# A long convolution and an MLP on one core: the opening laid out anew

## The chip, the cores and the metric

The kernel runs on one core of one Trainium2 chip. The metric is the device time of one execution in microseconds (us). TensorE is PE in the rows, its weight load PEld, VectorE is DVE, ScalarE is ACT, GpSimd is POOL, SyncE is SP.

## The reference

```python
h_filt = np.maximum(pos_emb @ w1, 0.0) @ w2 * np.exp(-0.01 * pos)[:, None]
u = x * v                                  # (4, 12480, 128)
L = 2 * S
y = irfft(rfft(u, n=L, axis=1) * rfft(h_filt, n=L, axis=0)[None], n=L, axis=1)[:, :S]
z = (x * y).reshape(B * S, D)              # 49920 tokens of 128
h = np.maximum(z @ w_in, 0.0)              # d_ff = 2048
out = (h * h) @ w_out
```

## The kernel before

The sequence is padded to 112 x 112 and the transforms become matrix products. For each of the four batches there are four stages. Stage one (`stage1`) multiplies x and v, folds the product into a sum half and a difference half (the tiles `ut`, three of them) and multiplies them by a small table; a step is four channels, and there are 32 steps. Its result is copied out of PSUM into the large tile `W` (`evac`). Stage two (`stage2`) multiplies each of 56 blocks of `W` by a table (`mm`), giving U in PSUM, and multiplies U by the filter's spectrum as complex numbers, in place in `W` (`post`). Stage three transforms back, 64 steps of two channels (`prep` gathers v out of `W`, `evac` copies to c and writes a sum and a difference into `W`). Stage four does the last transform, multiplies by x and writes z. Each matrix product over fp32 is one `matmul` and two instructions in the trace, in the first stage one for each half of the array's columns.

The filter goes ahead of the batches: an MLP (`filter_mlp`), then stages one and two with `b=None` and `filt=True`. Its spectrum goes through the tile `he` to the DRAM tensor `Hd`, 56 writes of 229 KB, and comes back as `ht` in the first batch's stage two. `Hd`, the inputs `xt` and `vt`, and the tables all go through SP's queue, in the order in which the program issues them.

The filter and the first batch run with `big=True` before the main loop. The other three batches run inside the main loop, spread between the products of the MLP with d_ff = 2048, by a generator from which `adv` takes steps. In the main loop each fp32 product is three of reduced operands: each factor is split into a high and a low part (`mm3`). The weights `w_in` and `w_out` are split the same way from 64-bit values by `convert_weights`, on VectorE with two casts on ScalarE for each piece.

Before the change: the tables of stage two are one tile of 56 blocks (`tabs[0]`), loaded in eight pieces of seven blocks, for the filter during its MLP, for the batch from the last steps of stage one on. The batch's stage one is started early by `step(s1)`: its loads stand at step 4 of the filter's stage one, its first folds three steps before the end of the filter's stage two. The weights are loaded and converted in eight pieces of 512 columns, one `step(conv)` after each step of the batch's stage three. Within each step of a stage the order on the engines is that of the program. `lag` is the number of steps by which `post` or `evac` follows `mm` (two, in stages two and three with `big`).

Of the kernel before, what the change touches and what calls it, by code (L numbers as in the profile page):

```python
# [16 lines left out]
D = 128  # L17
I = 112
# [13 lines left out]
TC = 7  # L32


@with_exitstack
def hyena_moe_kernel(
# [45 lines left out]
    def convert_weights(p, tp, dst):  # L82
        n = 512
        m = DFF // n
        V = nc.vector
        raws = []

        def load(c):
            if c < 2 * m:
                c0 = c % m * n  # L90
                src = w_in if c < m else w_out
                raw = p.tile([128, n, 2], I32, tag="raw", name="raw")
                nc.sync.dma_start(out=raw.rearrange("p a b -> p (a b)"), in_=src.bitcast(I32)[:, c0 * 2 : (c0 + n) * 2])
                raws.append(raw)

        load(0)
        for c in range(2 * m):
            c0, at = c % m * n, c // m * 2
            hi12, lo12 = dst[:, at, c0 : c0 + n], dst[:, at + 1, c0 : c0 + n]
            raw = raws.pop(0)  # L100
            low, high = raw[:, :, 0], raw[:, :, 1]

            def tmp(tag, dt=I32):
                return tp.tile([128, n], dt, tag=tag, name="cv", bufs=2)

            mag, top, sgn, rest = tmp("r", F32), tmp("gh"), tmp("gl"), tmp("r")
            yield
            V.tensor_scalar(out=top, in0=high, scalar1=0x7FFFFFFF, scalar2=None, op0=ALU.bitwise_and)
            V.tensor_scalar(out=mag, in0=top.bitcast(F32), scalar1=2.0**-15, scalar2=122880.0, op0=ALU.max, op1=ALU.min)
            yield  # L110
            V.tensor_scalar(out=top, in0=mag.bitcast(I32), scalar1=3, scalar2=0x7FFFFFFF, op0=ALU.logical_shift_left, op1=ALU.bitwise_and)
            V.tensor_scalar(out=sgn, in0=high, scalar1=-0x80000000, scalar2=0x40000000, op0=ALU.bitwise_and, op1=ALU.bitwise_xor)
            yield
            V.tensor_scalar(out=rest, in0=low, scalar1=1, scalar2=None, op0=ALU.logical_shift_right)
            load(c + 1)
            V.tensor_tensor(out=top, in0=top, in1=sgn, op=ALU.bitwise_xor)
            nc.scalar.copy(mag, rest)
            yield
            tf = top.bitcast(F32)
            V.tensor_scalar(out=sgn, in0=top, scalar1=-0x800000, scalar2=None, op0=ALU.bitwise_and)  # L120
            nc.scalar.copy(hi12, tf)
            yield
            V.scalar_tensor_tensor(out=mag, in0=mag, scalar=2.0**-51, in1=sgn.bitcast(F32), op0=ALU.mult, op1=ALU.mult)
            yield
            V.tensor_sub(out=tf, in0=tf, in1=hi12.bitcast(F32))
            yield
            V.tensor_add(out=lo12, in0=tf, in1=mag)
            yield
# [93 lines left out]
    def stage1(b, big, side="left", hook=None):  # L222
# [4 lines left out]
        with pool("s1", side) as p:  # L227
# [22 lines left out]
            def mul(t):  # L250
# [3 lines left out]
                if filt:  # L254
                    f = first_rows()[:, :, t * DC : (t + 1) * DC].rearrange("p j d -> p d j")
                    eng = nc.vector if t % 4 == 0 or t == 2 else nc.gpsimd
                    eng.tensor_add(out=ut[:, :, :gap], in0=f[:, :, HI:], in1=f[:, :, HI::-1])
                    eng.tensor_sub(out=ut[:, :, 64:], in0=f[:, :, HI + 1 :], in1=f[:, :, HI - 1 :: -1])
                else:
                    xt, vt = L[t]  # L260
                    (nc.vector if big else nc.gpsimd).tensor_mul(out=xt, in0=xt, in1=vt)
                    eng = nc.vector if big and t in (0, 2) else nc.gpsimd
# [20 lines left out]
            def evac(t, A):  # L283
                for h in range(DC // 2):
# [3 lines left out]
                    if big:  # L288
                        (nc.vector.tensor_copy if filt and h else nc.scalar.copy)(view, src)
# [41 lines left out]
    def table(src, k):  # L331
        nc.sync.dma_start(out=tabs[0][:, k * TC : (k + 1) * TC], in_=src[:, k * 2 * TC : (k + 1) * 2 * TC, :].rearrange("p (t k) m -> p t k m", k=2))

    def stage2(filt, big, side="left", hook=None):
# [3 lines left out]
        lh = 5 if big else 0  # L338
        T, Hs = {}, {}

        with pool("s2", side) as p:
# [7 lines left out]
            def load_h(t):  # L349
                if t >= n or filt:  # L350
                    return
                ht = p.tile([I, D, 2, 2], F32, tag="ht", name="ht", bufs=7 if big else 2)
                nc.sync.dma_start(out=ht, in_=Hd[:, t])
                Hs[t] = ht

            def mm(t):
                tb = tabs[0][:, t] if big else T.pop(t)
# [6 lines left out]
            def post(t, U):  # L364
                if filt:
                    he = p.tile([I, D, 4], F32, tag="he", name="he", bufs=4)
                    (nc.vector.tensor_copy if t % 2 else nc.scalar.copy)(he, U[:I].rearrange("p (c d) -> p d c", c=4))
                    nc.sync.dma_start(out=Hd[:, t].rearrange("p d k r -> p (d k r)"), in_=he.rearrange("p d c -> p (d c)"))
                    return
                ht = Hs.pop(t)  # L370
                Uv = U[:I].rearrange("p (k r d) -> p d k r", k=2, r=2)
                m = [
# [7 lines left out]
                eng = nc.vector if big and (t % 4 == 3 or t >= n - 3) else nc.gpsimd  # L380
                eng.tensor_add(out=im[0], in0=im[0], in1=re[1])
# [11 lines left out]
            for t in range(n + lag):  # L393
# [3 lines left out]
                yield 2  # L397
                if t - lag in prev:
# [12 lines left out]
    def stage3(big, ft=None, hook=None):  # L411
        n = D // 2
        with pool("s3") as p:
# [6 lines left out]
            def prep(t):  # L420
# [3 lines left out]
                (nc.gpsimd.tensor_copy if t % (5 if big else 3) == 2 else nc.scalar.copy)(q[t], by_channel(2 * t, 2 * t + 2))  # L424
# [15 lines left out]
            def evac(t, A):  # L440
# [4 lines left out]
                if big and t % 5 == 4:  # L445
                    nc.gpsimd.tensor_add(out=dst[:, 0, :, 1::-1], in0=c[:, :, 3:0:-2], in1=c[:, :, 0:3:2])
                else:
                    nc.vector.tensor_add(out=dst[:, 0, :, 1::-1], in0=q[:, :, 3:0:-2], in1=c[:, :, 0:3:2])
# [149 lines left out]
    ftp = take("ftp")  # L598
    tabs = [take("tbp", "right").tile([KP, NP, 2, I], F32, name="tbl", bufs=1)]

# [71 lines left out]
    def m_h(zT, f):  # L672
        A = psa.tile([128, 2, 512], F32, tag="A", name="A")
        for t in range(2):
            s = slice((2 * f + t) * 128, (2 * f + t + 1) * 128)
            mm3(A[:, t, :GT], (wi[0][:, s], wi[1][:, s]), zT)
# [34 lines left out]
    def m_o(i, f, hl):  # L711
# [4 lines left out]
        for t in range(2):  # L716
            s = slice((2 * f + t) * D, (2 * f + t + 1) * D)
            mm3(o, (wo[0][:, s], wo[1][:, s]), (hl[0][:, t, :], hl[1][:, t, :]), first=(f == 0 and t == 0), last=(f == NS - 1 and t == 1))
# [173 lines left out]
```

## Time and profile before

| what | us |
|---|---|
| median of 3 runs | 3220.01 (3218.57 to 3222.17) |
| the profiled execution | 3218.82 |
| its span | 3217.1 |
| filter MLP (0 to 43 us) | 43 |
| filter stage one (43 to 104) | 61 |
| filter stage two (104 to 153) | 49 |
| batch stage one (153 to 217) | 64 |
| batch stage two (217 to 310) | 93 |
| batch stage three (310 to 413) | 103 |
| start of stage four (413 to 428) | 15 |
| main loop and tail (from 428) | 2789 |

The stretches are cut by hand where the timeline changes from one stage to the next, to about a microsecond; neighbouring stages overlap a little there. In rows of the timeline the first number is the start in us from the span's begin, the second the duration.

### The profile page before, as it was taken

The numbers are of one execution on the slowest core, as the hardware profiler recorded it, in microseconds if no ns is written. First come the engines' busy times: TensorE is split into PE (matmuls) and PEld (weight loads), VectorE is DVE, ScalarE is ACT, GpSimd is POOL, SyncE is SP. The second block draws the span as 40 slices with busy tenths as digits, with TensorE's granted clock in tenths as the row PEclk, the third lists the DMA queues.
The fourth block names the chain that finished last, engine by engine and source line by source line (L and its number), as shares of the span: only waits on it lengthen the run. The fifth ranks groups of instructions, "written<-read, shape, count | busy, mean of one in ns | idle before, by whom it ended". The sixth has DMA issues, their size and how long they took to land.

```text
span 3217.1 us, 51651 instructions
## 1 busy us (share of the span) xinstructions
PE 3109.4 (97%) x17270; PEld 2850.4 (89%) x17270; DVE 2556.1 (79%) x3163; ACT 2412.2 (75%) x3273; POOL 1707.7 (53%) x1765
## 2 busy tenths in 40 slices
PE   8986789999999999999999999999999999999998
PEld 6754679999999999999999999999999999999998
DVE  6449779888887789888887789887887789877776
ACT  4330668778788878778788888778788888888886
POOL 6278956565655556655665566565655566200000
PEclk9999989999999999999999999999999999999999
DMA  5585156433410056534410056433420056300000
GB/s 143 176 214 156 54 126 159 133 97 114 122 58 19 22 138 156 134 100 114 121 56 18 18 138 158 133 104 110 119 64 20 22 125 156 75 25 24 24 26 18
DMA packets 330145, 304.75 MB, mean 95 GB/s; under 512 B 143784, under 2 KB 288472, under 8 KB 329880
## 3 DMA queue, kind: packets, MB, share of 16 engines
q1 hardware_dynamic: 301208, 256.48, 29.2%
q0 software_dynamic: 28672, 44.97, 6.1%
q8 instruction: 137, 2.24, 0.3%
q14 instruction: 128, 1.05, 0.1%
HBM read 215.09 MB, written 63.77 MB: 87 GB/s over the span
## 4 chain that ended last, share of the span: by engine, by line
PE 89%; POOL 3%; DVE 3%; issue 2%; DMA 2%; ACT 1%; SPq 0%; DVEq 0%; POOLq 0%; ACTq 0%
PE A L78 11%; PE A L80 11%; PE A L79 11%; PE O L79 9%; PE O L80 9%; PE O L78 9%; PE F L361 5%; PE F L437 5%; PE F L280 5%; PE F L79 4%; PE F L78 4%; PE F L80 4%; PE A L277 1%; DMA vt<-vs 1%; POOL W L449 1%
## 5 line engine op out<-in xcount | busy, mean ns | idle before, releaser
L687 ACT ACTIVATE r<-A 128x892 f32<-128x892 f32 x896 | 821.7, 917 | 309.5 <-PE A L80 298.8
L78 PE MATMUL A<-zh,wt 128*128 128x446 f32 x1792 | 715.9, 399 | 1.1 <-DVE gl L706 1.0
L706 DVE TENSOR_TENSOR gl<-r,gh 128x892 fp32r<-128x892 f32 x503 | 628.3, 1249 | 87.2 <-ACT r L694 73.6
L80 PE MATMUL A<-zh,wt 128*128 128x446 f32 x1792 | 651.3, 363 | 0.0
L79 PE MATMUL A<-zl,wt 128*128 128x446 f32 x1792 | 650.0, 363 | 0.0
L690 ACT ACTIVATE gh<-r 128x892 fp32r<-128x892 f32 x512 | 486.2, 950 | 141.8 <-PE O L80 128.2
L79 PE MATMUL O<-gl,wt 128*128 128x446 f32 x1440 | 523.8, 364 | 0.4 <-DVE gl L706 0.4
L80 PE MATMUL O<-gh,wt 128*128 128x446 f32 x1440 | 523.1, 363 | 0.0
L78 PE MATMUL O<-gh,wt 128*128 128x446 f32 x1440 | 522.8, 363 | 0.0
L694 ACT ACTIVATE r<-r 128x892 f32<-128x892 f32 x504 | 478.9, 950 | 14.6
L706 DVE TENSOR_TENSOR gl<-A,gh 128x892 fp32r<-128x892 f32 x392 | 426.0, 1087 | 73.6 <-ACT gh L690 55.6
L449 POOL TENSOR_TENSOR W<-c 112x224 f32<-112x224 f32 x256 | 329.9, 1294 | 289.1 <-ACT c L444 288.5
L692 DVE SCALAR_TENSOR_TENSOR A<-A,r 128x892 f32<-128x892 f32 x392 | 424.9, 1084 | 56.7 <-ACT r L687 55.0
L701 DVE CAST gh<-r 128x892 fp32r<-128x892 f32 x384 | 242.8, 632 | 248.5 <-ACT r L694 244.2
L654 POOL TENSOR_TENSOR zl<-zi,zh 128x446 fp32r<-128x446 f32 x111 | 132.4, 1193 | 522.7 <-PE A L80 381.8
L78 PEld LDWEIGHTS A<-zh,wt 128*128 128x128 f32 x1792 | 338.2, 189 | 26.5 <-DVE gl L706 2.6
L79 PEld LDWEIGHTS A<-zl,wt 128*128 128x128 f32 x1792 | 339.6, 190 | 19.6 <-DVE zl L654 0.2
L80 PEld LDWEIGHTS A<-zh,wt 128*128 128x128 f32 x1792 | 336.6, 188 | 22.8
L379 POOL TENSOR_TENSOR W<-W,m 112x256 f32<-112x256 f32 x224 | 217.0, 969 | 211.0 <-DVE m L377 185.1
L508 POOL TENSOR_TENSOR al<-W,ah 112x512 fp32r<-112x512 f32 x212 | 279.3, 1317 | 44.0 <-ACT ah L506 30.9
L79 PEld LDWEIGHTS O<-gl,wt 128*128 128x128 f32 x1440 | 271.8, 189 | 20.2 <-DVE gl L706 1.5
L78 PEld LDWEIGHTS O<-gh,wt 128*128 128x128 f32 x1440 | 270.4, 188 | 18.4
(117 smaller groups left out, 5675.8 us busy)
## 6 DMA issues: line engine op xcount, KB each, us to landing
ht<-Hd SPq DMA_DIRECT2D x224, 224.0 KB
tb<-t POOLq DMA_DIRECT2D x224, 196.0 KB, 3.3
xt<-xs SPq DMA_DIRECT2D x128, 196.0 KB
vt<-vs SPq DMA_DIRECT2D x128, 196.0 KB
xt<-x SPq DMA_DIRECT2D x224, 112.0 KB
out<-ot SPq DMA_DIRECT2D x112, 223.0 KB
tb<-t2s SPq DMA_DIRECT2D x168, 105.0 KB
zd<-zs SPq DMA_DIRECT2D x222, 64.0 KB
```

The source lines that it names most:

```text
L78: nc.tensor.matmul(o, lh, rh, start=first, stop=False)
L79: nc.tensor.matmul(o, lh, rl, start=False, stop=False)
L80: nc.tensor.matmul(o, ll, rh, start=False, stop=last)
L379: nc.gpsimd.tensor_sub(out=re[0], in0=re[0], in1=im[1])
L449: nc.gpsimd.tensor_sub(out=dst[:, 1], in0=c[:, :, 0:3:2], in1=c[:, :, 3:0:-2])
L508: eng.tensor_sub(out=lo, in0=w, in1=hi.bitcast(F32))
L687: nc.scalar.activation(r, h, AF.Relu)
L690: nc.scalar.activation(hi, r, AF.Square)
L692: nc.vector.scalar_tensor_tensor(out=h, in0=h, scalar=0.0, in1=r, op0=ALU.max, op1=ALU.mult)
L694: nc.scalar.activation(r, r, AF.Square)
L701: nc.vector.tensor_copy(hi, g)
L706: nc.vector.tensor_sub(out=lo, in0=g, in1=hi.bitcast(F32))
```

## The change

- `convert_weights`: the 16 pieces of 256 columns are loaded ahead, after the tables of the filter and before its stage one. They are converted in two interleaved chains, three instructions after each step of the filter's stage two. The result goes back into the memory of the raw pieces. Stage three no longer carries it.
- The table tile becomes two of 28 blocks, `tba` and `tbb`. The filter uses both; after its step 27 `tba` is given up and the batch's stage one takes its memory. The batch's stage two uses `tbb` as a ring of four pieces.
- Stage one with `big`: VectorE makes all folds, ScalarE all evacuations.
- Filter stage two: ScalarE makes all copies to `he`, which has three buffers in place of four.
- Batch stage two: ScalarE writes a turned copy of U (i times U) into PSUM, VectorE multiplies U by the real and the turned U by the imaginary part, GpSimd adds the two (VectorE for the last two). `ht` has five buffers in place of seven.
- Batch stage three: VectorE and ScalarE take turns in `prep`; VectorE makes all sums, GpSimd all differences.
- The load of `ft` moves to the front of the program.

```diff
+TH = 4
+CW = 256
+NCW = DFF // CW
...
-    def convert_weights(p, tp, dst):
-        n = 512
...
+    def load_weights(wp):
+        raws = []
+        for c in range(2 * NCW):
+            raw = wp.tile([128, CW, 2], I32, tag="w", name="raw", bufs=2 * NCW)
+            src = (w_in if c < NCW else w_out).bitcast(I32)[:, c % NCW * 2 * CW : (c % NCW + 1) * 2 * CW]
+            nc.sync.dma_start(out=raw.rearrange("p a b -> p (a b)"), in_=src)
+            raws.append(raw)
+        return raws
+
+    def convert_weights(p, wp, raws, wt, chunks):
+        for c in chunks:
+            low, high = raws[c][:, :, 0], raws[c][:, :, 1]
+            mag, top, sgn = (p.tile([128, CW], I32, tag=k, name="cv") for k in ("cm", "ct", "cs"))
+            mf = mag.bitcast(F32)
+            tf = top.bitcast(F32)
+            V.tensor_scalar(out=top, in0=high, scalar1=0x7FFFFFFF, scalar2=None, op0=ALU.bitwise_and)
+            V.tensor_scalar(out=mf, in0=tf, scalar1=2.0**-15, scalar2=122880.0, op0=ALU.max, op1=ALU.min)
+            V.tensor_scalar(out=top, in0=mag, scalar1=3, scalar2=0x7FFFFFFF, op0=ALU.logical_shift_left, op1=ALU.bitwise_and)
+            yield
+            V.tensor_scalar(out=mag, in0=low, scalar1=1, scalar2=None, op0=ALU.logical_shift_right)
+            nc.scalar.copy(mf, mag)
+            yield
+            wt[c] = wp.tile([128, 2, CW], F32R, tag="w", name="wt", bufs=2 * NCW)
+            hi12, lo12 = wt[c][:, 0, :], wt[c][:, 1, :]
+            V.tensor_scalar(out=sgn, in0=top, scalar1=-0x800000, scalar2=None, op0=ALU.bitwise_and)
+            yield
+            V.scalar_tensor_tensor(out=mf, in0=mf, scalar=2.0**-51, in1=sgn.bitcast(F32), op0=ALU.mult, op1=ALU.mult)
+            V.tensor_add(out=lo12, in0=tf, in1=mf)
...
                     f = first_rows()[:, :, t * DC : (t + 1) * DC].rearrange("p j d -> p d j")
-                    eng = nc.vector if t % 4 == 0 or t == 2 else nc.gpsimd
+                    eng = nc.vector
                     eng.tensor_add(out=ut[:, :, :gap], in0=f[:, :, HI:], in1=f[:, :, HI::-1])
                     eng.tensor_sub(out=ut[:, :, 64:], in0=f[:, :, HI + 1 :], in1=f[:, :, HI - 1 :: -1])
...
-                    eng = nc.vector if big and t in (0, 2) else nc.gpsimd
+                    eng = nc.vector if big else nc.gpsimd
                     eng.tensor_add(out=ut[:, :, :HI], in0=xt[:, :, :HI], in1=xt[:, :, HI:])
                     eng.tensor_sub(out=ut[:, :, 64:], in0=xt[:, :, :HI], in1=xt[:, :, HI:])
...
                     if big:
-                        (nc.vector.tensor_copy if filt and h else nc.scalar.copy)(view, src)
+                        nc.scalar.copy(view, src)
...
-    def table(src, k):
-        nc.sync.dma_start(out=tabs[0][:, k * TC : (k + 1) * TC], in_=src[:, k * 2 * TC : (k + 1) * 2 * TC, :].rearrange("p (t k) m -> p t k m", k=2))
+    def table(src, k, half):
+        nc.sync.dma_start(
+            out=half[:, k % TH * TC : (k % TH + 1) * TC],
+            in_=src[:, k * 2 * TC : (k + 1) * 2 * TC, :].rearrange("p (t k) m -> p t k m", k=2),
+        )
...
-        lh = 5 if big else 0
-        T, Hs = {}, {}
+        lh = 4 if big else 0
+        T, Hs, iUs, two = {}, {}, {}, {}
...
-                ht = p.tile([I, D, 2, 2], F32, tag="ht", name="ht", bufs=7 if big else 2)
+                ht = p.tile([I, D, 2, 2], F32, tag="ht", name="ht", bufs=5 if big else 2)
                 nc.sync.dma_start(out=ht, in_=Hd[:, t])
...
-                tb = tabs[0][:, t] if big else T.pop(t)
+                tb = tabs[filt and t < TH * TC][:, t % (TH * TC)] if big else T.pop(t)
...
-                    he = p.tile([I, D, 4], F32, tag="he", name="he", bufs=4)
-                    (nc.vector.tensor_copy if t % 2 else nc.scalar.copy)(he, U[:I].rearrange("p (c d) -> p d c", c=4))
+                    he = p.tile([I, D, 4], F32, tag="he", name="he", bufs=3)
+                    nc.scalar.copy(he, U[:I].rearrange("p (c d) -> p d c", c=4))
                     nc.sync.dma_start(out=Hd[:, t].rearrange("p d k r -> p (d k r)"), in_=he.rearrange("p d c -> p (d c)"))
...
+                if big:
+                    w = W[:I, t].rearrange("p (d k r) -> p d k r", k=2, r=2)
+                    m = p.tile([I, D, 2, 2], F32, tag="m1", name="m1")
+                    iv = iUs.pop(t)[:I].rearrange("p (k r d) -> p d k r", k=2, r=2)
+                    nc.vector.tensor_mul(out=w, in0=Uv, in1=ht[:, :, :, 0:1].to_broadcast([I, D, 2, 2]))
+                    nc.vector.tensor_mul(out=m, in0=iv, in1=ht[:, :, :, 1:2].to_broadcast([I, D, 2, 2]))
+                    (nc.vector if t >= n - 2 else nc.gpsimd).tensor_add(out=w, in0=w, in1=m)
+                    return
...
-                eng = nc.vector if big and (t % 4 == 3 or t >= n - 3) else nc.gpsimd
-                eng.tensor_add(out=im[0], in0=im[0], in1=re[1])
+                nc.gpsimd.tensor_add(out=im[0], in0=im[0], in1=re[1])
+
+            def turn(t, U):
+                if filt or not big:
+                    return
+                if t % 2 == 0:
+                    two[0] = psa.tile([128, 2, 512], F32, tag="A", name="A")
+                iU = iUs[t] = two[0][:, t % 2, :]
+                u, iu = (x[:I].rearrange("p (k r d) -> p k r d", k=2, r=2) for x in (U, iU))
+                nc.scalar.mul(iu[:, :, 0], u[:, :, 1], -1.0)
+                nc.scalar.copy(iu[:, :, 1], u[:, :, 0])
...
+                if t - 1 in prev:
+                    turn(t - 1, prev[t - 1])
                 if t - lag in prev:
                     post(t - lag, prev.pop(t - lag))
                 yield 3
...
-                (nc.gpsimd.tensor_copy if t % (5 if big else 3) == 2 else nc.scalar.copy)(q[t], by_channel(2 * t, 2 * t + 2))
+                copy = (nc.vector.tensor_copy if t % 2 else nc.scalar.copy) if big else nc.gpsimd.tensor_copy if t % 3 == 2 else nc.scalar.copy
+                copy(q[t], by_channel(2 * t, 2 * t + 2))
...
                 nc.scalar.copy(c, q)
-                if big and t % 5 == 4:
-                    nc.gpsimd.tensor_add(out=dst[:, 0, :, 1::-1], in0=c[:, :, 3:0:-2], in1=c[:, :, 0:3:2])
-                else:
-                    nc.vector.tensor_add(out=dst[:, 0, :, 1::-1], in0=q[:, :, 3:0:-2], in1=c[:, :, 0:3:2])
+                nc.vector.tensor_add(out=dst[:, 0, :, 1::-1], in0=q[:, :, 3:0:-2], in1=c[:, :, 0:3:2])
                 nc.gpsimd.tensor_sub(out=dst[:, 1], in0=c[:, :, 0:3:2], in1=c[:, :, 3:0:-2])
...
-    ftp = take("ftp")
-    tabs = [take("tbp", "right").tile([KP, NP, 2, I], F32, name="tbl", bufs=1)]
...
-        if c == I // 8 - 3:
-            for k in range(NP // TC):
-                table(t2h, k)
-
-    s1f = stage1(None, True, "left", lambda t: t == -28 and step(s1))
-    s2f = stage2(True, True, "left", lambda t: t == NP - 3 and step(s1))
-    s1 = stage1(0, True, "right", lambda t: step(s2) if t == -3 else t in (-24, -16, -8) and table(t2s, t // 8 + 3))
+
+    def during_s2f(t):
+        if t == NP // 2 - 1:
+            held["tba"].close()
+        if t in (NP // 2, NP - 3):
+            step(s1)
+        step(conv[t % 2], 3)
+
+    def during_s1(t):
+        if t in (-20, -8):
+            table(t2s, t // 12 + 2, tabs[0])
+        if t == -3:
+            step(s2)
+
+    def during_s2(t):
+        if t == 0:
+            for k in (2, 3):
+                table(t2s, k, tabs[0])
+        if t % TC == 0 and TH <= t // TC + 3 < NP // TC:
+            table(t2s, t // TC + 3, tabs[0])
+
+    ft = load_f(take("ftp"))
+    s1f = stage1(None, True, "left")
     filter_mlp(tables)
+    wp = ctx.enter_context(pool("wp", "right"))
+    wt = {}
+    tabs = [take(k, "right").tile([KP, TH * TC, 2, I], F32, name=k, bufs=1) for k in ("tbb", "tba")]
+    for k in range(2 * TH):
+        table(t2h, k, tabs[k < TH])
+    raws = load_weights(wp)
     run(s1f)
-    run(s2f)
-    s2 = stage2(False, True, "left", lambda t: t % TC == 0 and 3 <= t // TC + 2 < NP // TC and table(t2s, t // TC + 2))
-    ft = load_f(ftp)
+    s1 = stage1(0, True, "right", during_s1)
+    cvp = take("cvp")
+    conv = [convert_weights(cvp, wp, raws, wt, range(k, 2 * NCW, 2)) for k in range(2)]
+    run(stage2(True, True, "left", during_s2f))
+    for x in conv:
+        run(x)
+    held["cvp"].close()
+    s2 = stage2(False, True, "left", during_s2)
     run(s1)
     run(s2)
-    held["tbp"].close()
+    held["tbb"].close()
 
     mp = ctx.enter_context(pool("mp", "right"))
-    wt = mp.tile([128, 4, DFF], F32R, name="wt", bufs=1)
-    wi, wo = (wt[:, 0, :], wt[:, 1, :]), (wt[:, 2, :], wt[:, 3, :])
     s4 = stage4(0, done, take("t1p"))
-    cwp = take("cwp", bufs=1)
-    conv = convert_weights(cwp, mp, wt)
-    next(conv)
-    
-    def during(t):
-        step(conv)
-        if t == -12:
-            step(s4)
-
-    run(stage3(True, ft, during))
-    run(conv)
-    held["cwp"].close()
+    run(stage3(True, ft, lambda t: t == -12 and step(s4)))
+
+    def wi(k, h, f):
+        return wt[k * NCW + f // 2][:, h, f % 2 * 128 : (f % 2 + 1) * 128]
...
```

The products of the main loop take their weights from the 16 tiles through `wi(k, h, f)`.

## Rows read from the trace of the kernel before

**Rows 1.** Stretches: length, then PE, PEld, DVE, ACT, POOL busy, clock, DMA, GB/s.
```profile
43.00:104.00 61.00, 53.50 (x512) 39.31 (x512) 32.98 (x49) 16.98 (x31) 43.24 (x49) 0.97 0.29 70
104.00:153.00 49.00, 47.68 (x221) 38.97 (x222) 20.06 (x31) 16.36 (x28) 0.00 (x0) 1.00 0.73 241
153.00:217.00 64.00, 54.32 (x491) 38.99 (x491) 26.17 (x35) 30.58 (x61) 44.09 (x59) 0.96 0.93 247
217.00:310.00 93.00, 65.19 (x253) 39.82 (x249) 81.84 (x122) 1.96 (x4) 78.30 (x95) 0.97 0.63 168
310.00:413.00 103.00, 68.88 (x512) 63.91 (x512) 74.32 (x138) 63.78 (x130) 86.22 (x95) 0.87 0.17 49
413.00:428.00 15.00, 8.93 (x36) 7.65 (x37) 7.09 (x15) 5.54 (x12) 4.55 (x9) 0.53 0.37 99
```

**Rows 2.** Timeline of the filter's stage one, VectorE's folds and PE.
```profile
45.04 0.67 DVE L257 TENSOR_TENSOR ut<-W 112x228 f32<-112x228 f32 x1
45.63 0.66 DVE L258 TENSOR_TENSOR ut<-W 112x224 f32<-112x224 f32 x1
...
50.71 0.35 PE L277 MATMUL A<-ef,ut 112*64 112x224 f32 x1
...
50.90 0.35 PE L277 MATMUL A<-ef,ut 112*64 112x224 f32 x1
...
71.51 1.09 DVE L257 TENSOR_TENSOR ut<-W 112x228 f32<-112x228 f32 x1 [0.50 <-PE A L278]
```

**Rows 3.** Waits in the filter's stage one: sum, times, longest.
```profile
PE A L277 <- DVE W L289: 5.9, 7, 1.1
```

**Rows 4.** The chain of waits in the filter's stage two.
```profile
105.32 20.99 PE F L361 x96
...
143.90 0.70 DVE he L367
144.62 2.64 DMA Hd<-he
```

**Rows 5.** Groups by shape, 0 to 480 us: busy us, mean ns, idle before.
```profile
L444 ACT COPY c<-A 112x448 f32<-112x448 f32 x64 | 34.0, 533 | 25.8 <-PE A L437 8.7 <-POOL W L449 6.9 <-DVE W L448 5.9
L448 DVE TENSOR_TENSOR W<-A,c 112x224 f32<-112x224 f32 x52 | 29.3, 564 | 28.7 <-ACT c L444 27.4
L424 ACT COPY v<-W 112x448 f32<-112x448 f32 x51 | 28.9, 570 | 93.2 <-POOL W L379 93.2
...
L508 POOL TENSOR_TENSOR al<-W,ah 112x512 fp32r<-112x512 f32 x17 | 22.4, 1319 | 3.1 <-ACT ah L506 2.0
...
L367 ACT COPY he<-F 112x512 f32<-112x512 f32 x28 | 16.4, 586 | 33.0 <-PE F L361 20.8 <-DMA Hd<-he 12.3
```

**Rows 6.** Conversion's instructions: ns min/median/max, first and last start.
```profile
L108 DVE TENSOR_SCALAR cv<-raw x8: 407/416/529, 313.9 to 397.7; 128x512 int32<-128x512 int32 x8
...
L117 ACT CAST cv<-cv x8: 618/618/619, 320.7 to 403.1; 128x512 f32<-128x512 int32 x8
...
L127 DVE TENSOR_TENSOR wt<-cv x8: 668/768/1034, 325.6 to 408.1; 128x512 fp32r<-128x512 f32 x8
```

**Rows 7.** Batch stage one: a wait, and the product in the timeline.
```profile
DVE xt L261 <- DMA vt<-vs: 32.7, 20, 6.3
...
151.42 0.61 DVE L261 TENSOR_TENSOR xt<-xt,vt 112x448 f32<-112x448 f32 x1
```

**Rows 8.** Batch stage two: the second product's ns, then two in the timeline.
```profile
L377 DVE TENSOR_TENSOR m<-F,ht x56: 672/680/692, 223.7 to 312.8; 112x512 f32<-112x512 f32 x56
...
257.33 0.67 DVE L377 TENSOR_TENSOR m<-F,ht 112x512 f32<-112x512 f32 x1
257.93 0.67 DVE L377 TENSOR_TENSOR W<-F,ht 112x512 f32<-112x512 f32 x1
```

**Rows 9.** Batch stage three: POOL's difference (ns), PE's densest piece.
```profile
L449 POOL TENSOR_TENSOR W<-c x63: 655/855/2149, 319.6 to 412.6; 112x224 f32<-112x224 f32 x63
...
327.13 2.73 PE L437 MATMUL A<-ft,v 112*112 112x112 f32 x24 [0.86 <-POOL v L424]
```

More of the change, by code (lines that the diff above doesn't have):

```diff
@@ L80, in mm3 @@
         nc.tensor.matmul(o, ll, rh, start=False, stop=last)
-    def convert_weights(p, tp, dst):
-        n = 512
-        m = DFF // n
-        V = nc.vector
[L86 to L106, printed above, removed]
+    def load_weights(wp):
[6 more added lines that the diff above has]
+        return raws
@@ L107, in convert_weights @@
+    def convert_weights(p, wp, raws, wt, chunks):
+        V = nc.vector
+        for c in chunks:
[4 more added lines that the diff above has]
+            V.tensor_scalar(out=top, in0=high, scalar1=0x7FFFFFFF, scalar2=None, op0=ALU.bitwise_and)
             yield
-            V.tensor_scalar(out=top, in0=high, scalar1=0x7FFFFFFF, scalar2=None, op0=ALU.bitwise_and)
@@ L109, in convert_weights @@
-            V.tensor_scalar(out=mag, in0=top.bitcast(F32), scalar1=2.0**-15, scalar2=122880.0, op0=ALU.max, op1=ALU.min)
+            V.tensor_scalar(out=mf, in0=tf, scalar1=2.0**-15, scalar2=122880.0, op0=ALU.max, op1=ALU.min)
             yield
-            V.tensor_scalar(out=top, in0=mag.bitcast(I32), scalar1=3, scalar2=0x7FFFFFFF, op0=ALU.logical_shift_left, op1=ALU.bitwise_and)
+            V.tensor_scalar(out=top, in0=mag, scalar1=3, scalar2=0x7FFFFFFF, op0=ALU.logical_shift_left, op1=ALU.bitwise_and)
@@ L112, in convert_weights @@
+            yield
+            V.tensor_scalar(out=mag, in0=low, scalar1=1, scalar2=None, op0=ALU.logical_shift_right)
+            nc.scalar.copy(mf, mag)
+            yield
             V.tensor_scalar(out=sgn, in0=high, scalar1=-0x80000000, scalar2=0x40000000, op0=ALU.bitwise_and, op1=ALU.bitwise_xor)
             yield
-            V.tensor_scalar(out=rest, in0=low, scalar1=1, scalar2=None, op0=ALU.logical_shift_right)
-            load(c + 1)
             V.tensor_tensor(out=top, in0=top, in1=sgn, op=ALU.bitwise_xor)
-            nc.scalar.copy(mag, rest)
@@ L118, in convert_weights @@
-            yield
-            tf = top.bitcast(F32)
-            V.tensor_scalar(out=sgn, in0=top, scalar1=-0x800000, scalar2=None, op0=ALU.bitwise_and)
+            wt[c] = wp.tile([128, 2, CW], F32R, tag="w", name="wt", bufs=2 * NCW)
+            hi12, lo12 = wt[c][:, 0, :], wt[c][:, 1, :]
             nc.scalar.copy(hi12, tf)
             yield
-            V.scalar_tensor_tensor(out=mag, in0=mag, scalar=2.0**-51, in1=sgn.bitcast(F32), op0=ALU.mult, op1=ALU.mult)
+            V.tensor_scalar(out=sgn, in0=top, scalar1=-0x800000, scalar2=None, op0=ALU.bitwise_and)
@@ L126, in convert_weights @@
             yield
-            V.tensor_add(out=lo12, in0=tf, in1=mag)
+            V.tensor_add(out=lo12, in0=tf, in1=mf)
             yield
@@ L674, in m_h @@
         for t in range(2):
-            s = slice((2 * f + t) * 128, (2 * f + t + 1) * 128)
-            mm3(A[:, t, :GT], (wi[0][:, s], wi[1][:, s]), zT)
+            mm3(A[:, t, :GT], (wi(0, 0, 2 * f + t), wi(0, 1, 2 * f + t)), zT)
         return A
@@ L716, in m_o @@
         for t in range(2):
-            s = slice((2 * f + t) * D, (2 * f + t + 1) * D)
-            mm3(o, (wo[0][:, s], wo[1][:, s]), (hl[0][:, t, :], hl[1][:, t, :]), first=(f == 0 and t == 0), last=(f == NS - 1 and t == 1))
+            mm3(o, (wi(1, 0, 2 * f + t), wi(1, 1, 2 * f + t)), (hl[0][:, t, :], hl[1][:, t, :]), first=(f == 0 and t == 0), last=(f == NS - 1 and t == 1))
         if f == NS - 1:
```

## The prediction

> **What bounds the kernel now.** I read the page first: PE is busy in 97% of the span, and the second part of the page shows only the first five or six slices thinner. So I cut the span at the changes of stage in the timeline and asked for the busy time of each stretch [rows 1]. They are, in order, the filter's stage one (43 to 104 us), its stage two (to 153), the first batch's stage one (to 217), two (to 310) and three (to 413), and the start of stage four before the main loop (to 428). What follows is one dense TensorE stream that the change leaves alone. The opening is 428 us, and only there can the time move. The reader is to see in [rows 1] that each stretch has another limit. For each I then read groups by shape, waits, chain and timeline.
>
> - Filter stage one, 61 us: PE pairs start 0.19 us apart [rows 2], so 32 x 8 pairs are 48.6 us. 12.4 us are lost. Of these 5.9 us, seven times 0.84, are PE waiting for an evacuation on VectorE [rows 3], which stands in its queue behind a fold.
> - Filter stage two, 49 us: the chain is one run of PE (96 instructions in 20.99 us, so 224 are 49.0 us), later a ring of VectorE copy 0.70 and write of Hd 2.64 us [rows 4]. With four buffers that ring is (0.70 + 2.64 + some 0.1) / 4 = 0.86 us, PE's step is 4 x 0.219 = 0.87. Both limits lie on each other.
> - Batch stage one, 64 us: DMA busy 0.93 at 247 GB/s [rows 1], VectorE waits 32.7 us for the second input [rows 7].
> - Batch stage two, 93 us: VectorE 81.8 and POOL 78.3 busy. The second product comes 56 times from 223.7 to 312.8 us: 1.62 us a step [rows 8].
> - Batch stage three, 103 us: POOL 86.2 busy, DVE 74.3, PE 68.9 at a granted clock of 0.87 [rows 1]. Nothing is full. Conversions, copies and folds of three engines wait for each other.
>
> **The change part by part.**
>
> *Filter MLP.* The load of ft now stands ahead of the first loads on SP. An issue there is of the order of 0.4 us: +0.4. The t2h tables go after the MLP instead of inside it, half of them and the 16 weight chunks into memory that the MLP leaves. That is 6 + 4.2 MB behind the MLP's end. At the 247 GB/s of [rows 1] it takes some 42 us, and stage one, in which the queue moved 70 GB/s, covers it. If it didn't, the second half of the tables would be late only from step 28 of stage two on. Counted at nothing.
>
> *Filter stage one.* All folds go to VectorE, all evacuations to ScalarE. The add took 0.67 us without POOL beside it, the sub came 0.59 us after it, and beside POOL the add took 1.09 [rows 2]. POOL has no work now, so a step's folds are some 1.25 us, under PE's 8 x 0.19 = 1.52. Two evacuations at 0.55 (near the 0.533 of a copy of the same size, [rows 5]) are 1.1 us on ScalarE, also under it. So PE sets the step. Bounds: the named 5.9 us, or all 12.4 lost. I take 8, since the start and the last evacuation stay: **-8**.
>
> *Filter stage two.* Three things are added. (a) The ring has three buffers, and ScalarE alone fills it at 0.586 us [rows 5]. A turn is 0.586 + 2.64 + 0.1 = 3.33 us, over three buffers 1.11 a step in place of 0.87. With three writes in flight in place of four the landing may be shorter. At 2.0 us the step would be 0.90. I take 1.06. (b) Conversion: ten VectorE instructions a chunk, whose medians at 512 columns run from 0.416 to 0.768 us and sum to 6.2, in the presence of POOL [rows 6]. Halved in width, 16 chunks are at least 16 x 6.2 / 2 = 49 us, and with 0.05 us more for each instruction's fixed part 58. Over the 54 steps in which the hook has work left that is 0.9 to 1.07 us a step, no more than the ring, and POOL is silent. ScalarE has 32 casts of about 0.35 (half of 0.618, [rows 6], and a rest): 11 us beside 56 x 0.586 = 33, so 44 in all. But its casts queue behind copies that wait for a write, so VectorE follows the ring's pace. (c) At step 28 batch stage one starts: ef and eight loads, 1.8 MB, go into SP's queue ahead of the next writes of Hd. At 247 GB/s that holds them 7 us. One turn of the ring hides some, so 3 us are added. Together 56 x 1.06 + 3 = 62 against 49: **+13**. Bounds: 56 x 0.90 = 50 and 56 x 1.11 + 7 = 69, so +1 to +20.
>
> *Batch stage one.* In before, this stretch carries 247 GB/s x 64 us = 15.8 MB. One table of 0.75 MB goes to the later stage, and one write of Hd and one load of ht fewer fall in it: about 1.2 MB, 5 us. The product on VectorE takes 0.61 us without POOL [rows 7] and the two folds about 0.3 to 0.6 each, so 1.2 to 1.8 us a step, under the 2.0 of now, and SP waits less for POOL's folds. **-5**. Bounds: 0 if the ring of inputs gives nothing, -12 if the step falls near PE's 1.52 plus start.
>
> *Batch stage two.* VectorE loses 16 adds; its products start 0.60 us apart [rows 8], so 1.20 us a step. POOL's two strided operations of 256 become one dense add of 512. POOL's subtraction of 512 took 1.319 [rows 5]. The lower bound of a step is VectorE's 1.20, the upper 1.50 (the 0.655 of a POOL add of 224, [rows 9], by width). I take 1.31. ScalarE turns U in two instructions of 256 from PSUM to PSUM. No row has ScalarE writing PSUM: between half of 0.533 and 0.586 each, and I take 0.4, nearer to half the size; 0.8 a step lies under POOL's 1.31 even at the upper bound of 1.17. The turned U comes a step before its use. Loads of ht have five buffers for seven, so each has some four steps, 5.2 us, to land; a table of 0.75 MB (3 us) ahead of it in SP's order leaves 2.2 us. Six tables stand in this stretch, two of them together: I count 3 us of stalls, bounds 0 and 15. So 56 x 1.31 + 3 + 1 for the first turn = 77 against 93: **-16** (-4 to -22).
>
> *Batch stage three.* Conversion leaves, the half-way adds of POOL (12) and copies of POOL (13) go to VectorE. Per step now: ScalarE 0.533 + 0.570 / 2 = 0.82, VectorE 0.564 + half a copy (0.57 as on ScalarE) = 0.85 [rows 5], POOL one sub of 0.655 to 0.855 [rows 9], PE 8 x 0.11 = 0.88 (24 instructions in 2.73 us at the best [rows 9]). Four engines at the same pace don't reach it. I take 1.0, and 7 us for the start at a low clock and the last steps: 64 + 7 = 71 against 103: **-32** (-24 at 1.13, -38 at 0.9).
> In before POOL's sub took 0.655 us at the least and 2.149 at the longest [rows 9], with VectorE instructions on SBUF beside it. The Trainium skill (SBUF — State Buffer, SBUF: two separate sides) says that VectorE in its two-port mode and GpSimd exclude each other at a shared port pair, and names the fp32 copy within SBUF as such an operation. It speaks against moving the copy v to VectorE. By that rule a pair of steps is 2 x 0.66 + 0.57 = 1.9 us on that port, 0.95 a step, and by the row without it 0.88. My 1.0 holds for both.
>
> *Sum:* 0.4 - 8 + 13 - 5 - 16 - 32 = -47.6. The profiled execution took 3218.8 us (span 3217.1), 1.2 under the median of 3220.0. So 3218.8 - 47.6 + 1.2 = **3172**.
>
> **Rivals.**
> - *Stage three keeps waiting.* The start of the conversion is gone, but ScalarE still must copy c before VectorE's add and POOL's sub, and VectorE's copies keep POOL out. At 1.25 us a step: 80 + 7 = 87, 16 more than forecast, 3188. For it: in before no engine was full there. Against it: the work that goes is VectorE's 52 us and a quarter of POOL's.
> - *The ring costs nothing.* Landing near 2.0 us and the casts hidden: stage two at 51, 11 less, 3161. For it: the 2.64 us were seen at DMA busy 0.73 [rows 1]. Against: its share hardly falls, and the input loads come on top.
> - *Tables stall stage two.* Each of six costs 2.5 us: 15 in place of 3, 3184. For it: five buffers for seven. Against: no wait for ht ranks in before.
> - *Slower.* Place: the filter's stage two. Loads and writes share SP's order, and if a turn of the three-buffer ring grows to twice, all three engines hang on it. The other parts give 61 us, so it decides from 49 + 61 = 110 us on, 1.96 a step, a turn of 5.9 us. For it: VectorE waited 32.7 us for loads where DMA was at 0.93. Against: here DMA is at 0.73, and the loads are 1.8 MB in one burst. At 115 us: 3225.
>
> **How the numbers follow.** Forecast 0.58, stage three waits 0.17, ring free 0.13, tables stall 0.06, slower 0.06 (half of it within 0.2%). 0.2% is 6.4 us, about what a measurement of this kernel can tell from no change. Faster 0.94, same 0.03, slower 0.03. The forecast's own range is 3161 to 3183, from the bounds of the single terms, which hardly fall on one side together. The range goes down to 3155, most of the free ring's case, and up to 3194, over stage three waiting by its own spread.
>
> **What would show it.** In the changed profile: filter stage one some 53 us with PE in front and no wait for VectorE. Stage two about 62, ScalarE's copies waiting for Hd. Batch stage one 59, still at about 0.93 DMA. Stage two 77 with a POOL add of 1.3 us as the repeating link. Stage three 71, PE clock above 0.87. The prediction is wrong if the ring takes more than 1.2 us a step, if POOL's dense add takes 1.5, or if stage three stays over 1.2.

## The result, and the profile after

The changed kernel took 3188.28 us (3181.39 to 3189.73, 4 runs) against 3221.09 for the kernel before (3218.57 to 3223.11, 4 runs): ratio 0.9894, interval 0.9877 to 0.9911, 33 us less. The forecast was 3172, 16 us too low. The time lies above the forecast's own range (3161 to 3183) and inside the wider one, which goes up to 3194 for a rival's sake. The profiled execution, at 3181.4 us the fastest of the four, has a span of 3179.6 us.

To compare the stages I cut both traces at the same marks: the first fold of the filter, the first product of its stage two, the first batch product of stage one, the first of stage two, the first copy v, and the first cast of stage four. Between these marks the stretches are not quite those of [rows 1], which were cut by hand. Microseconds between marks:

| stage | before | changed | difference | forecast |
|---|---|---|---|---|
| start to first fold | 42.4 | 42.5 | +0.1 | +0.4 |
| filter one | 62.9 | 52.7 | -10.2 | -8 |
| filter two | 48.6 | 65.4 | +16.8 | +13 |
| batch one | 68.0 | 59.6 | -8.4 | -5 |
| batch two | 93.1 | 79.4 | -13.7 | -16 |
| batch three | 99.6 | 77.9 | -21.7 | -32 |
| stage four and main loop | 2802.5 | 2802.1 | -0.4 | 0 |

The windows of the changed kernel at these marks, columns as in [rows 1]:

```profile
42.50:95.20 52.70, 50.91 (x513) 39.37 (x513) 41.74 (x69) 31.86 (x64) 0.00 (x0) 0.97 0.49 138
95.20:160.60 65.40, 56.79 (x226) 37.86 (x226) 51.10 (x164) 40.47 (x86) 0.34 (x3) 0.95 0.67 212
160.60:220.20 59.60, 52.30 (x513) 40.16 (x512) 37.00 (x89) 33.04 (x67) 0.00 (x0) 0.97 1.00 260
220.20:299.70 79.50, 63.37 (x224) 37.53 (x224) 69.92 (x115) 39.78 (x113) 66.67 (x54) 0.94 0.75 196
299.70:377.50 77.80, 61.61 (x512) 56.98 (x512) 50.82 (x96) 49.01 (x97) 45.01 (x67) 0.97 0.04 11
```

Filter one is now limited by PE, busy 50.9 of 52.7 us, where it had 53.5 of 62.9 between the same marks. Batch one is limited by DMA, share 1.00 where it was 0.89. In batch three no engine is busy for 80% of the time. That is what remains to be explained there.

The chain of waits in filter two of the changed kernel (its longest pieces, in order of time; a line "DMA Hd<-he" is a write from its issue to its landing):

```profile
117.82 0.59 ACT he L366
118.43 2.35 DMA Hd<-he
120.88 0.59 ACT he L366
121.49 2.40 DMA Hd<-he
123.99 0.59 ACT he L366
125.44 1.30 SPq L242
130.13 5.57 DMA Hd<-he
135.80 0.59 ACT he L366
136.44 4.44 PE F L360 x11
```

A turn is 120.88 - 117.82 = 3.06 us for three buffers. Over the eight turns from 98.53 to 123.99 us it is 3.18, or 1.06 a step, in place of [rows 4]'s ring of four beside PE's 0.87. From 125.00 on the inputs of batch one enter SP's queue. Their nine issues alone take SP until 130.03, some 0.42 us each and one 1.30; the next write is issued at 130.13 and lands 5.57 us later, in place of 2.4. PE stands still for 6.8 us. Between 136 and 141 us its granted clock is then 0.57, and eleven product instructions take 4.44 us, where [rows 4] has 0.219 for each. The waits name the same place: between the marks ScalarE waits 22.8 us for writes of Hd, the longest 7.0.

```profile
ACT he L366 <- DMA Hd<-he: 22.8, 37, 7.0
```

GpSimd's adds in batch two, merged in the timeline (start, length, number, idle time before and its releaser):

```profile
223.93 14.84 POOL L377 TENSOR_TENSOR W<-W,m 112x512 f32<-112x512 f32 x12 [99.75 <-DVE m L376]
240.44 2.49 POOL L377 TENSOR_TENSOR W<-W,m 112x512 f32<-112x512 f32 x2 [1.67 <-DVE m L376]
243.57 2.49 POOL L377 TENSOR_TENSOR W<-W,m 112x512 f32<-112x512 f32 x2 [0.64 <-PE F L360]
246.99 12.35 POOL L377 TENSOR_TENSOR W<-W,m 112x512 f32<-112x512 f32 x10 [0.92 <-DVE m L376]
261.24 8.64 POOL L377 TENSOR_TENSOR W<-W,m 112x512 f32<-112x512 f32 x7 [1.91 <-DVE m L376]
271.28 25.85 POOL L377 TENSOR_TENSOR W<-W,m 112x512 f32<-112x512 f32 x21 [1.40 <-DVE m L376]
```

The last piece is 25.85 / 21 = 1.23 us a step. Before it stand five gaps, 1.67 + 0.64 + 0.92 + 1.91 + 1.40 = 6.5 us. The six tables are issued between 214.4 and 262.7 us, and after 271.28 there is no gap.

### The profile page after: what moved, and what is told of

Read it like the earlier page. It is cut to its first block, busy times and chain, and to the rows that moved or that the text cites. A ratio compares the mean times of both kernels' runs of the same rounds, so it can differ in the third digit from the quotient of the medians.

```text
span 3179.6 us, 51832 instructions
## 1 busy us (share of the span) xinstructions
PE 3103.8 (98%) x17270; PEld 2840.2 (89%) x17270; DVE 2570.1 (81%) x3319; ACT 2475.1 (78%) x3442; POOL 1561.5 (49%) x1592
## 4 chain that ended last, share of the span: by engine, by line
PE 90%; DMA 3%; DVE 2%; ACT 2%; POOL 1%; issue 1%; SPq 0%; ACTq 0%; DVEq 0%; POOLq 0%
PE A L81 11%; PE A L83 11%; PE A L82 11%; PE O L82 9%; PE O L83 9%; PE O L81 9%; PE F L456 5%; PE F L360 5%; PE F L276 5%; PE F L82 4%; PE F L81 4%; PE F L83 4%; PE A L273 2%; DMA Hd<-he 1%; PE A L456 1%
## 5 line engine op out<-in xcount | busy, mean ns | idle before, releaser
L465 POOL TENSOR_TENSOR W<-c 112x224 f32<-112x224 f32 x256 | 309.2, 1208 | 311.8 <-ACT c L463 311.6
L83 PEld LDWEIGHTS O<-gh,wt 128*128 128x128 f32 x1440 | 269.9, 187 | 18.8
L81 PEld LDWEIGHTS O<-gh,wt 128*128 128x128 f32 x1440 | 270.4, 188 | 18.2
```

The source lines that it names most:

```text
L81: nc.tensor.matmul(o, lh, rh, start=first, stop=False)
L83: nc.tensor.matmul(o, ll, rh, start=False, stop=last)
L465: nc.gpsimd.tensor_sub(out=dst[:, 1], in0=c[:, :, 0:3:2], in1=c[:, :, 3:0:-2])
```

## The experiments

The stages by the same marks (us), and each run's time. One profile each; the changed kernel was profiled twice. Where the time is not called a median it is that of a single execution, and the argument goes by the stages.

| run | filter one | filter two | batch one | batch two | batch three | time |
|---|---|---|---|---|---|---|
| changed, first profile | 52.7 | 65.4 | 59.6 | 79.4 | 77.9 | 3181.4 |
| changed again | 52.7 | 65.9 | 63.5 | 80.2 | 78.3 | 3186.5 median |
| c: five buffers | 52.7 | 65.3 | 59.8 | 81.8 | 78.2 | 3184.2 |
| a PSUM tile a step | 52.7 | 65.2 | 63.2 | 81.1 | 61.7 | 3170.6 |
| he: four buffers | 51.0 | 58.8 | 58.1 | 80.0 | 78.1 | 3173.3 |
| inputs spread | 52.7 | 63.4 | 61.8 | 81.3 | 78.3 | 3185.0 |
| tables by block, late | 51.0 | 65.5 | 66.6 | 100.0 | 78.7 | 3211.3 |
| conversion after | 51.0 | 64.7 | 117.3 | 80.1 | 78.6 | 3240.9 |
| U not turned | 52.7 | 65.4 | 63.4 | 93.2 | 78.2 | 3202.9 |
| stage three's old engines | 52.7 | 65.6 | 61.4 | 81.0 | 76.3 | 3183.9 |
| tables by block, ahead | 51.0 | 64.8 | 63.1 | 74.2 | 78.1 | 3182.8 |
| together | 52.7 | 57.3 | 62.1 | 73.6 | 59.7 | 3152.4 median |
| before, folds alone | 51.0 | 49.0 | 62.7 | 93.5 | 99.6 | 3204.5 |

**The changed kernel again.** No edit.

> The changed kernel once more, unchanged. Its four times lay at 3181 and 3187 to 3190 us, and the one profile is of the fastest. If the 7 us between them lie in the stretches where the DMA queue is the limit (batch stage one at a DMA share of 1.00, filter stage two), another profile shows them there: batch stage one near 64 us in place of 59.6, or filter stage two near 70 in place of 65.4. If they lie in the main loop, the opening ends again at 391.5 us and the rest is longer.

The time was 3186.49 us (3185.23 to 3187.66; ratio 0.9888, interval 0.9871 to 0.9904). The profile's opening ends 5.5 us later, 3.9 of it in batch one, and from its end on the trace is 2802.9 us long against 2802.1. So the difference between executions lies in the opening, mostly where the DMA share is near 1. Over the runs in which batch one has the same instructions (all but "conversion after" and "before, folds alone") it lies between 58.1 and 66.6 us; smaller differences in that column say nothing by themselves.

**Batch three: the ring of c, or the shared PSUM tile.** The chain of the changed kernel repeats this every 4.58 us (the next first copy starts at 335.70):

```profile
331.10 0.54 ACT c L463
331.71 0.69 POOL W L465
332.40 0.54 ACT c L463
332.97 0.62 DVE W L464
333.73 1.89 PE A L456 x16
```

There are two PSUM tiles for A, each for a pair of steps, and this is the way round of one of them: PE fills it in 1.89 us, ScalarE and VectorE empty its halves one behind the other, and only then does PE get it back (PE waits 30 times for VectorE's sum). Two tiles in turn give a pair of steps every 2.29 us.

```profile
PE A L456 <- DVE W L464: 12.9, 30, 0.7
```

ScalarE's second copy, at 332.40, starts when GpSimd's difference ends. But a sum of VectorE ends at 332.32, and the compiled program has this order (the numbers count each engine's finished instructions):

```
ScalarE copy c (first of a pair)    waits PE 1034,    Pool 92   -> ScalarE 406
VectorE sum from it                 waits ScalarE 406           -> DVE 514
ScalarE copy c (second of a pair)   waits DVE 514,    Pool 93
```

Pool 93 was given out three steps earlier. What the second copy waits for is the sum of the first half of the same PSUM tile. Two runs tell the ring of c and the shared tile apart.

```diff
-                c = p.tile([I, 2, 4, HI], F32, tag="c", name="c", bufs=lag + 1)
+                c = p.tile([I, 2, 4, HI], F32, tag="c", name="c", bufs=lag + (3 if big else 1))
```

> Batch stage three with five buffers for c in place of three; all else as changed. The profile puts ScalarE's second copy of each pair of steps down to GpSimd's difference just before it, which would be the ring of c. If that is so, the pair of steps falls from 2.29 us to some 2.0 and the stage from 77.8 us to about 68. Rival, from the program's own waits: that copy waits for VectorE's sum of the step before, since both steps of a pair lie in one PSUM tile. Then more buffers for c change nothing: 77.8 us, within 1.

78.2 us: no change, so the ring of c is not it.

```diff
-                if big:
-                    if t % 2 == 0:
-                        two[0] = psa.tile([128, 2, 512], F32, tag="A", name="A")
-                    A = two[0][:, t % 2, :]
+                if big and t % 2 == 0:
+                    A = psa.tile([128, 2, 512], F32, tag="A", name="A")[:, 0, :]
                 else:
                     A = bank()
```

> Batch stage three with a PSUM tile of its own for each step (even steps in the two-bank tiles, odd steps in a bank of the pool of three), c's ring as changed. If the shared tile makes ScalarE's second copy wait for VectorE's first sum, the pair of steps falls from 2.29 us to 1.9 or 2.0, PE's 1.88 or VectorE's 1.8 of work, and the stage from 77.8 to 65 to 69 us. If the ring of c is the cause, it stays at 77.8.

61.7 us, 16 less, better than expected. In the timeline of this run PE's steps stand 0.83 us apart, back to back:

```profile
330.77 0.99 PE L454 MATMUL A<-ft,v 112*112 112x112 f32 x8
...
331.60 0.99 PE L454 MATMUL F<-ft,v 112*112 112x112 f32 x8
...
332.43 0.99 PE L454 MATMUL A<-ft,v 112*112 112x112 f32 x8
```

This run undoes two ties at once: ScalarE's second copy no longer waits for VectorE's first sum, and PE gets a step's tile back without its neighbour (there are also five places for a step in place of four). The first tie holds at most 0.76 us of the 4.58 (331.64 to 332.40), which would leave 1.9 us a pair; so it is not the whole of the 16 us. What each is worth alone was not run.

The shared tile was there before the change too; there the conversion stood in front of it, as the run with stage three's old engines shows below.

**Filter two: the ring of he.**

```diff
-                    he = p.tile([I, D, 4], F32, tag="he", name="he", bufs=3)
+                    he = p.tile([I, D, 4], F32, tag="he", name="he", bufs=4)
...
-    ft = load_f(take("ftp"))
...
     held["cvp"].close()
+    ft = load_f(take("ftp"))
```

> The filter's stage two with four buffers for he in place of three; ft is loaded after that stage to make room. If the ring sets its step, (0.59 + 2.45 + 0.1) / 4 = 0.79 us lies under PE's 0.87, so steps go at 0.87 to 0.9 outside the burst, and the stage falls from 65.4 us to some 55. If the conversion beside it sets the step (51 us of VectorE's work, and casts in ScalarE's queue), it falls by less than 4 us. The burst of loads in the middle stays in either case, some 6 us.

58.8 us, 6.6 to 7.1 less, not the ten expected. The stop in the middle stays whole, as said (ScalarE waits 6.9 us there); but outside it ScalarE still waits 5.7 us for writes, so four buffers do not quite free the ring either.

```profile
ACT he L366 <- DMA Hd<-he: 12.6, 14, 6.9
```

**The conversion out of the way.** `step(conv[t % 2], 3)` is deleted from `during_s2f`; the chains then run at once behind the stage.

> The conversion is taken out of the steps of the filter's stage two and runs by itself after it, with the batch's first folds ahead of it in the queue. Only the length of the filter's stage two is read from this run. If the ring of he sets its step, it stays at 63 to 66 us without the conversion. If the conversion holds ScalarE's copies up, it falls to 58 or less.

64.7 us. VectorE has 4.6 us of work in that stage in place of 51.1, and the stage is shorter by 0.7 to 1.2. So the conversion is all but free there, and together with the run with four buffers this says that the ring sets the step.

**The burst of inputs.**

```diff
             for t in range(early):
                 load(t)
+                if big and not filt and t < early - 1:
+                    yield 1
...
-        if t in (NP // 2, NP - 3):
+        if t in (NP // 2, NP // 2 + 6, NP // 2 + 12, NP // 2 + 18, NP - 3):
             step(s1)
```

> The first four pairs of inputs of the batch are loaded one pair at a time, at steps 28, 34, 40 and 46 of the filter's stage two, in place of all eight loads at step 28. If the burst in the queue costs the 6.8 us for which PE stood still at 129.7 us, that stop goes and each pair costs under 1 us: the stage falls from 65.4 to about 60 us. If the bytes themselves cost the time, whatever their order, it stays within 2 us of 65.4.

63.4 us, about 2 less: nearer to the second reading. The stop of 6.8 us is gone (the longest wait for a write is 2.0), but between the marks the waits for Hd are still 20.1 us in sum, against 22.8. With three buffers in the ring, writes that start and land a little later among the loads cost at each turn most of what the burst cost at once.

```profile
ACT he L368 <- DMA Hd<-he: 20.1, 36, 2.0
```

Whether the place in SP's queue or the bytes beside the writes cost more was not told apart: no run issued the inputs from another queue.

**Batch two: tables.** First three blocks in four steps:

```diff
-        if t == 0:
-            for k in (2, 3):
-                table(t2s, k, tabs[0])
-        if t % TC == 0 and TH <= t // TC + 3 < NP // TC:
-            table(t2s, t // TC + 3, tabs[0])
+        for b in range(2 * TC + 3 * t // 4, min(2 * TC + 3 * (t + 1) // 4, NP)):
+            s = b % (TH * TC)
+            nc.sync.dma_start(out=tabs[0][:, s : s + 1], in_=t2s[:, 2 * b : 2 * b + 2, :].rearrange("p (t k) m -> p t k m", k=2))
```

> In batch stage two the six tables of seven blocks are loaded block by block, three blocks in four steps, in place of 0.75 MB at a time. If the stops before 271 us come from a table standing ahead of ht in the queue, the stage goes at GpSimd's 1.23 us a step throughout: 56 x 1.23 + 3.5 = 72 to 74 us in place of 79.5. Rival: 16.4 MB in 70 us are 234 GB/s, close to the 260 of the stage before, and the ring of five is short at that load: then the stops are spread but stay, 77 us or more.

The order is at fault in this run: the lead of 14 blocks is used up by the end, and the last block is issued after its product, which used an older one. 100.0 us says nothing on the question. But its middle does: 27 adds in one piece, then pairs with waits of 6 us.

```profile
244.88 33.37 POOL L377 TENSOR_TENSOR W<-W,m 112x512 f32<-112x512 f32 x27 [0.27 <-issue]
...
312.56 2.48 POOL L377 TENSOR_TENSOR W<-W,m 112x512 f32<-112x512 f32 x2 [6.13 <-DVE m L376]
```

With `5 * t // 6` in place of `3 * t // 4`:

> As the run with tables block by block, but five blocks in six steps, so that the last block is issued six steps ahead of its product. In the run before, 27 GpSimd adds went without a stop from 244.9 to 278.3 us while three blocks in four steps came in, and the stage was long only where the blocks came too late. If pieces of 0.75 MB make the stops, the stage now takes 72 to 75 us in place of 79.4 to 81.8. If the load as a whole does (107 KB and 229 KB a step are 260 GB/s or so), it stays at 78 or more.

74.2 us, and the adds run in two pieces:

```profile
225.67 18.51 POOL L377 TENSOR_TENSOR W<-W,m 112x512 f32<-112x512 f32 x15 [102.86 <-DVE m L376]
244.63 48.26 POOL L377 TENSOR_TENSOR W<-W,m 112x512 f32<-112x512 f32 x39 [0.45 <-DVE m L376]
```

Pieces of 0.75 MB ahead of ht in the queue made the stops: 5.2 to 7.6 us against the runs with whole tables and a turned U. The run's one time, 3182.8 us, hardly shows it: from stage four on its trace is 2806.8 us long, some 4 us more than in most other runs, for which no cause was found.

**U not turned.** `post` as before, `turn` returns at once, the placing of loads as changed.

> Batch stage two as before (VectorE's two products of U, two strided operations that GpSimd and VectorE share), with all else as changed, the five buffers for ht and the placing of the tables among it. If the turned U is what shortened the stage, it goes at 1.62 us a step again and takes 91 to 95 us, and the tables hide behind the slower pace. If the new placing of loads did it, it stays under 85.

93.2 us, the 93.1 of before: the whole gain of this stage comes from the turned U, and the new placing of loads costs nothing at the slower pace.

**Stage three with the old engines.** `prep` and `evac` as before, no conversion.

> Batch stage three with the engines of before (GpSimd takes every fifth copy v and every fifth sum, ScalarE the other copies), but still without the conversion; all else as changed. If the gain of 22 us there comes from the conversion's leaving, the stage takes 74 to 82 us, as with the change. If the new share of the engines brings it, the stage takes 90 us or more.

76.3 us. The new share of the engines brings nothing here. The conversion's leaving, with the loads of its pieces, brings it all. GpSimd is busy 57 us in this run, in place of 86 [rows 1].

**Before, with the folds alone.** The three engine choices of `stage1` put into the kernel before.

> The kernel before with one part of the change alone: in stage one VectorE makes all folds and ScalarE all evacuations. By the prediction's reason (PE waits for an evacuation behind a fold in VectorE's queue) the filter's stage one falls from 62.9 to 52 to 54 us. The batch's stage one, 68.0 us, falls by under 3 us if the DMA queue is its limit (the three tables are still in it), and to 62 or less if GpSimd's folds held back the loads.

Filter one 51.0 us. Batch one 62.7 with all three tables still in it, 5.3 less than before: at the limit between the two readings, and no more than that stage's spread. The waits say more than the length. Before, SP waited 16.2 us for GpSimd's folds before it could issue loads; here it waits 3.7 us for VectorE's, and the queue carries 257 GB/s where it was 238. So GpSimd's folds had held back some of the loads. (3204.49 us in one execution.) First before, then this run, between the marks:

```profile
SPq L246 <- POOL ut L264: 16.2, 19, 1.5
153.90:221.90 68.00, 57.27 (x513) 41.86 (x512) 25.27 (x33) 32.10 (x65) 44.79 (x60) 0.95 0.89 238
...
SPq L246 <- DVE ut L264: 3.7, 9, 0.4
143.30:206.00 62.70, 54.09 (x513) 41.40 (x513) 39.64 (x93) 32.13 (x65) 0.00 (x0) 0.95 0.98 257
```

**Together.** PSUM tile for each step, four buffers for he (and `ft` loaded later, as above), inputs spread, tables by block ahead.

> Together: a PSUM tile for each step in batch stage three, four buffers for he, inputs spread over four steps of the filter's stage two, tables block by block ahead. Filter stage two: 58.8 us was measured with four buffers and the burst of loads; without the burst some 53 to 55, since a ring of four leaves slack for it, where with three it gave 2 us. Batch stage two 73 to 80, batch stage three 62. Against the changed kernel (3186 us): -16 for stage three, -11 for filter stage two, -0 to -7 for the tables, so 3152 to 3160 us. If the inputs' bytes cost the same in any order, filter stage two stays at 58 and the sum is 3157 to 3164.

3152.38 us (3148.51 to 3154.78, 5 runs), ratio to before 0.9782, interval 0.9769 to 0.9795: twice the gain of the change. Filter two is 57.3, so with four buffers too the spread inputs give only 1.5 us and the second reading of that stage holds. What the 8 us over PE's 49 are was not tried further; ScalarE still waits 11.6 us for writes there.

## Why the prediction came out as it did

- *Filter one, -8.* Right in mechanism, small by 2. PE waits no longer for an evacuation on VectorE, and the part alone in the kernel before gives 51.0 us (in the runs of the changed kernel the stage takes 52.7 or 51.0).
- *Filter two, +13.* The ring is right: a step of 1.06 forecast, 1.06 measured over eight turns before the burst. The conversion is hidden as said (51.1 us of VectorE against 49 to 58). Too small is the term (c) for the burst: 3 us, with "one turn of the ring hides some". 56 steps at 1.06 are 59.4 us and the stage took 65.4, so the burst cost 6, with one wait of 7: a ring already without slack has nothing to hide with. The term was also worked out from the bytes alone; what held the write back first were SP's nine issues, 5.0 us, then its own longer landing, and PE came back at a lower clock. So +16.8 in place of +13. The rival "the ring costs nothing" falls.
- *Batch one, -5.* -4.5 and -8.4 in two profiles. I gave the fewer bytes as the cause, and the run with the folds alone gives 5.3 us with all tables in place. The cause that the waits show is the one I named second, SP waiting for GpSimd's folds (16.2 us before). How the gain is shared between it and the moved table is not shown: both shares are less than the stage's own spread, from 58.1 to 66.6 us.
- *Batch two, -16.* The steady step was better than forecast (1.23 against 1.31), the stalls larger (6.5 us in the main part against 3). I had six tables at half a microsecond each, since a load has "some four steps to land"; the five gaps in the adds are 0.6 to 1.9 us each. That the two errors nearly cancel is luck. The rival of the tables had the right mechanism; its 15 us were twice too many.
- *Batch three, -32.* This term makes most of the miss: -21.7. The conversion's leaving is the cause of the gain, as said. Of the 10.3 us, 3.4 are the base (103 us in the hand-cut stretch, 99.6 between the marks), and the 7 us for the two ends were some 2.5 too many; the rest, 9.4, is the step. "Four engines at the same pace don't reach it. I take 1.0" stood on busy times alone; the step was 1.15. I had not looked at what a copy waits for inside the pair: two steps share a PSUM tile, ScalarE's second copy is tied to VectorE's first sum, and PE gets the tile back only behind the second sum. With a tile for each step the four engines do reach 0.83, which is PE's own pace (the prediction had 0.88 for it). The rival "stage three keeps waiting" named a chain over c between three engines and a size of 1.25. Its copy and sum do stand in the loop, at 1.15 a step; the run with more buffers for c rules the ring of c out.
- *The shared port.* By that rule of the Trainium skill (SBUF — State Buffer, SBUF: two separate sides) a pair of steps could not go under 1.9 us. The run with a PSUM tile a step does two steps in 1.66 with the copies v on VectorE beside GpSimd, so the estimate that I drew from it was too high. Its 0.57 was ScalarE's time for the copy; VectorE's first two, with GpSimd idle, took 0.38 and 0.39 us. With these the same sum is 1.7, so the run does not decide on the rule itself.
- *Sum.* Against the profile (-37.4) the miss is 10 us, and it is stage three's. The other terms miss by -2.2, +3.8, -3.4 and +2.3, which cancel by luck. It is luck too that the median agrees with the 3188 of the rival "stage three keeps waiting": that rival had 87 us in the stage, which took 77.9; the median comes to 3188 because the other executions were slower than the profiled one. None of the three signs of a wrong prediction came: the ring's step is 1.06, the dense add at most 1.30, stage three's step 1.15. The medians of the changed kernel lie 5 to 7 us above that profile, in the DMA-bound part of the opening.

## What to carry to other kernels

Busy times of four balanced engines give a floor, not a pace: before trusting it, read for each instruction of the loop which instruction of the step before it waits for, and look for tiles that two steps share. When a ring is cut to the length at which it sets the pace, transfers put into the same queue are paid for nearly in full: spreading them gave back 2 us of some 6 here. Count the slack first, and count the issues as well as the bytes. Large loads ahead of a short ring are paid for at each load, and cutting them into pieces of a step's size gave the stage's time back here, if the lead holds to the last piece.

## What was not expected of the hardware

GpSimd's add of 112x512 took 1.25 to 1.30 us beside VectorE's products, steady at 1.23 from start to start. ScalarE's turn from PSUM to PSUM, 112x256, took 0.361 and 0.349 us, under the 0.4 I had taken. VectorE's copy v of 448 columns took 0.38 and 0.39 us at the start of stage three, where GpSimd was idle, and has a median of 0.527 over the stage. Where the profile puts a wait down to the engine that ended last, the program named another engine that had ended 0.07 us earlier; only the program's own wait and an experiment told them apart. Nine DMA issues in a row held SP for 5.0 us. And at a DMA share of 0.95 to 1.04 the same instructions took 58 to 67 us from run to run.
